# A new fixed instruction order for a fused attention and MLP-mixer kernel, made with another accounting of DMA transposes

## The chip, the core and the metric

The kernel runs on one core of a Trainium2 chip. The core has five engines that work side by side, each with an instruction queue of its own that it follows strictly in order: TensorE (PE, matrix products and transposes by the identity), VectorE (DVE), ScalarE (ACT), GpSimd (POOL) and SyncE (SP, here only for issuing transfers). Engines wait for each other by semaphores. 16 DMA engines move the data; transfers are issued by SP (queue q1 in the profile) and by POOL (queue q0). The metric is the device time of one launch in microseconds (us). Before the change the median of three runs is 201.78 us (201.45 to 202.1).

## The reference

One sequence of 2048 rows with 448 columns (bf16) goes through two blocks. LN is a layer norm without weights, over the columns of a row.

```python
# block A: 16 heads of 28 columns; each row attends to itself and to 7 earlier rows, 2 apart
off = jnp.arange(8) * 2
idx = pos[:, None] - off[None, :]                  # masked where negative
q, k, v = split(LN(x) @ wqkv)                      # 448 -> 3 x 448
logits = einsum("bhsd,bhswd->bhsw", q, k[idx]) * 28 ** -0.5
h = x + einsum("bhsw,bhswd->bhsd", softmax(logits), v[idx]) @ wo
# block B, on y = LN(h)
g = gelu(LN(y) @ w1)                               # four column quarters, shifted by +1, -1, +2, -2 rows
x1 = y + concat(shifted quarters of g) @ w2
out = h + x1 + gelu(LN(x1) @ w3) @ w4              # 448 -> 1792 -> 448
```

## The kernel before

The 2048 rows are 16 tiles of 128 rows, and these are four groups t = 0 to 3 of four tiles. Everything lives on the chip between the loads of x and the stores of the result. The phases of one group, as the code names them:

- N1 t: statistics and normalization of four tiles of x, into a buffer `lntm` (rows on the partitions; the last 64 columns are copied once more, "doubled", so that the columns fill 512).
- A1 t: `transposed` turns the buffer so that the columns lie on the partitions (`actT`), then products with wqkv give q and k. V t: products for v, evicted to `vt`; POOL then issues the copies vwp, vwa, vwb and vwc, which rearrange `vt` into the windows `vw`.
- A2 t: DVE multiplies q by shifted k (`qk_r`), PE sums over each head with a 0/1 matrix (`zc`). S t: softmax on DVE and ACT (`mx`, `ls`, `zs`, result `pb`), then PE transposes `pb`.
- A3 t: DVE builds band matrices `bd_r` from the attention weights, PE multiplies them by the `vw` windows. O t: products with wo and the residual x, written over `xin`.
- B1 t: normalization of the normalized row (two layer norms in one step), a turn, and as M t the products with w1 with gelu.
- B2 u, T u, W3 u, B3 u: products with w2, residual and layer norm; the turn; products with w3 with gelu (`h3T`); products with w4 and the store. These go by five units u of 3, 4, 4, 4 and 1 tiles.

A turn is done in one of two ways. The strings in `TURN` say which, one letter per group or unit:

- `t` (`transposed_pe`): 16 PE transposes of 128x128 by the identity, in two lots of eight, and two ACT copies of 128x1024 out of the accumulators.
- `d` (`dma_turn`): one DMA transpose, issued on SP's queue, from `lntm` to `actT`. The profile calls it `actT<-lntm`, DMA_TRANSPOSE. Before the change there are nine.

The weights w3 (1344 KB and two of 224 KB) and w4 (1568 KB) are loaded by POOL. `LOADS = '01'` puts the issue of w3 behind the last copy of V 0 and that of w4 behind the last copy of V 1, in POOL's queue only; they wait for nothing else.

The order of the work is written out. The list `ORDER` holds the number of each operation (1084 before). `_Sched.schedule` goes once through it, models a start and an end for each operation and appends it to its engine's queue. The modelled times decide only which buffer a tile gets and where filler products go on PE; what stays of the list on the chip is each engine's own order and the semaphore waits for data and buffers. Two operations on different engines keep no order of the list between them, unless one waits for the other. An edge in `op.odeps` (`behind=`) means "later in the list" and makes no wait where the engines differ or no data pass. In the model a turn is a transfer without bytes on SP, while loads and copies hold `dma_free`, the time at which modelled transfers have moved. The model also knows that certain DVE instructions and POOL's additions (`block`) delay one another.

In the profile every instruction of the program has the line 1050, where `emit_engine` calls the method of the engine (1054 in the changed kernel), so that rows are told apart by the names of their tiles: `actT<-lntm` is a turn, `arena<-in_B_w_dram` a load of a weight of block B, `vw<-vt` a copy for V, `arena<-arena,xin` on POOL the addition of the two residuals, `lntm<-xin,nm,rs_y` on DVE a normalization of bf16 rows, `ps<-ident` on PE a filler product.

Of the kernel before, what the change touches and what calls it, by code (L numbers as in the profile page):

```python
# [6 lines left out]
ALU = mybir.AluOpType  # L7
# [6 lines left out]
TURN = {'A1': 'ttdd', 'B1': 'dddd', 'B2': 'tdddt'}  # L14
NORM = {'N0': 'vavv', 'N1': 'avvv', 'B1': 'avva', 'B2': 'vaavv'}
# [6 lines left out]
    0, 9, 8, 6, 10, 1, 2, 3, 11, 4, 35, 22, 36, 5, 37, 12, 23, 38, 13, 24, 14, 25, 39, 15, 26, 46, 16, 40, 27, 52, 17, 28, 41, 53, 47, 18, 29, 55,  # L22
    48, 66, 19, 30, 42, 56, 54, 49, 20, 31, 67, 60, 57, 68, 43, 21, 32, 58, 33, 50, 61, 34, 44, 69, 51, 62, 59, 70, 63, 104, 45, 105, 64, 106, 72,
    108, 65, 73, 7, 112, 107, 111, 109, 74, 110, 75, 113, 71, 144, 142, 145, 114, 115, 124, 116, 76, 122, 117, 77, 78, 118, 120, 119, 121, 123, 148,
    143, 146, 79, 80, 81, 82, 83, 149, 147, 125, 84, 150, 126, 85, 151, 154, 155, 86, 152, 153, 87, 88, 89, 90, 91, 92, 127, 129, 133, 135, 131, 93,
    94, 130, 156, 95, 96, 140, 138, 173, 128, 161, 157, 204, 132, 205, 137, 189, 190, 248, 191, 194, 196, 250, 192, 206, 162, 163, 134, 280, 281,
    207, 282, 139, 136, 159, 158, 164, 287, 160, 195, 174, 285, 172, 209, 165, 193, 249, 166, 211, 169, 167, 170, 288, 286, 283, 175, 251, 168, 208,
    210, 171, 197, 284, 347, 252, 176, 212, 255, 97, 98, 99, 100, 101, 102, 103, 289, 199, 200, 201, 290, 254, 256, 177, 221, 219, 198, 253, 217,
    178, 257, 258, 226, 215, 260, 259, 218, 222, 141, 213, 216, 261, 179, 220, 262, 180, 263, 351, 350, 348, 349, 264, 214, 352, 181, 356, 227, 361,
    357, 359, 182, 183, 440, 369, 184, 354, 353, 225, 368, 355, 265, 185, 187, 358, 186, 188, 370, 362, 360, 372, 373, 375, 363, 224, 376, 228, 266,  # L30
    374, 231, 229, 234, 444, 232, 237, 230, 240, 267, 365, 223, 371, 233, 235, 242, 241, 236, 238, 243, 244, 294, 202, 377, 292, 203, 239, 364, 296,
    246, 268, 245, 291, 379, 247, 298, 300, 295, 299, 301, 297, 442, 269, 443, 441, 270, 303, 309, 304, 302, 381, 305, 307, 366, 445, 312, 306, 313,
    308, 271, 446, 382, 452, 454, 450, 314, 272, 315, 447, 451, 310, 560, 559, 316, 273, 317, 383, 453, 448, 367, 449, 274, 275, 561, 564, 384, 276,
    278, 457, 455, 566, 277, 279, 456, 563, 385, 319, 458, 567, 318, 327, 320, 330, 386, 321, 328, 387, 325, 388, 322, 323, 326, 333, 331, 324, 389,
    397, 336, 398, 378, 293, 380, 401, 329, 390, 334, 399, 391, 339, 335, 332, 392, 337, 393, 395, 400, 402, 394, 341, 343, 403, 396, 420, 342, 338,
    406, 404, 405, 345, 423, 421, 426, 424, 422, 407, 461, 408, 432, 425, 344, 565, 340, 410, 411, 409, 346, 427, 434, 412, 429, 428, 418, 416, 419,
    459, 460, 463, 436, 417, 430, 465, 488, 433, 489, 466, 464, 462, 467, 543, 562, 437, 431, 490, 491, 492, 497, 499, 470, 435, 471, 468, 469, 473,
    474, 494, 475, 476, 501, 438, 477, 544, 478, 498, 495, 503, 504, 505, 493, 496, 500, 502, 506, 439, 507, 518, 545, 522, 510, 509, 519, 546, 516,
    514, 512, 508, 520, 745, 515, 746, 479, 547, 480, 513, 481, 511, 521, 548, 523, 483, 517, 482, 486, 487, 549, 761, 747, 570, 311, 524, 568, 484,
    529, 531, 569, 415, 414, 572, 485, 550, 530, 748, 551, 576, 573, 528, 574, 413, 532, 577, 472, 533, 578, 575, 525, 749, 750, 751, 579, 580, 552,  # L40
    571, 526, 581, 584, 553, 762, 752, 753, 754, 755, 756, 757, 758, 763, 764, 765, 766, 767, 768, 554, 583, 582, 555, 557, 585, 556, 586, 535, 534,
    769, 536, 770, 777, 778, 779, 780, 771, 558, 590, 594, 661, 538, 587, 541, 772, 781, 664, 667, 542, 588, 539, 540, 589, 782, 773, 783, 774, 537,
    632, 668, 633, 784, 593, 592, 591, 670, 638, 636, 669, 595, 599, 662, 637, 600, 663, 634, 639, 677, 635, 665, 785, 640, 644, 666, 786, 673, 678,
    671, 759, 674, 675, 601, 676, 642, 672, 643, 641, 787, 602, 712, 775, 603, 645, 714, 604, 646, 605, 606, 610, 612, 608, 679, 614, 680, 613, 611,
    607, 615, 718, 716, 713, 715, 616, 719, 717, 720, 721, 617, 722, 623, 625, 620, 609, 649, 621, 618, 624, 650, 788, 789, 627, 619, 622, 726, 628,
    876, 908, 909, 860, 910, 630, 892, 861, 862, 893, 877, 911, 878, 912, 894, 913, 879, 863, 790, 880, 914, 864, 733, 725, 626, 724, 731, 723, 647,
    732, 651, 895, 896, 915, 916, 881, 730, 631, 653, 629, 648, 654, 734, 897, 898, 899, 735, 652, 655, 917, 865, 866, 867, 882, 900, 901, 868, 883,
    884, 885, 918, 869, 870, 871, 919, 886, 887, 888, 889, 902, 903, 904, 905, 737, 598, 597, 596, 791, 736, 776, 660, 792, 738, 727, 890, 920, 921,
    741, 891, 657, 728, 743, 872, 740, 873, 744, 739, 742, 681, 874, 682, 683, 684, 690, 922, 875, 760, 686, 685, 687, 797, 799, 795, 692, 688, 691,
    689, 906, 798, 796, 793, 800, 694, 794, 695, 801, 696, 697, 802, 803, 703, 701, 804, 699, 693, 704, 705, 849, 805, 707, 708, 698, 706, 702, 956,  # L50
    940, 806, 807, 924, 850, 810, 811, 809, 972, 973, 974, 941, 957, 925, 975, 958, 959, 960, 942, 943, 961, 962, 944, 926, 927, 945, 976, 977, 928,
    946, 710, 700, 851, 808, 812, 729, 816, 852, 815, 813, 658, 709, 711, 817, 907, 923, 527, 656, 659, 963, 929, 947, 978, 948, 979, 930, 931, 964,
    932, 933, 980, 981, 982, 983, 984, 934, 935, 985, 965, 936, 818, 937, 938, 986, 853, 854, 855, 987, 939, 949, 950, 819, 820, 966, 821, 967, 829,
    825, 827, 951, 952, 830, 822, 826, 828, 823, 824, 831, 832, 968, 833, 834, 838, 839, 840, 837, 841, 842, 953, 969, 844, 954, 970, 845, 836, 846,
    843, 835, 1020, 1068, 1021, 988, 1052, 1022, 989, 1023, 1024, 1004, 1005, 990, 1053, 1036, 1006, 991, 1007, 1069, 1037, 1038, 1008, 1054, 1055,
    1009, 992, 1056, 1057, 1010, 1039, 993, 1058, 1040, 1041, 1011, 1012, 1059, 1013, 1060, 1042, 1025, 1026, 1027, 994, 995, 1014, 1015, 847, 848,
    1028, 996, 1029, 1030, 1016, 857, 814, 1017, 1070, 1018, 971, 1019, 955, 1031, 997, 998, 1032, 1033, 999, 1034, 1000, 1061, 1001, 1071, 1072,
    1062, 1063, 1064, 1043, 1044, 1035, 1045, 1002, 1046, 1065, 1066, 1047, 1048, 1049, 1050, 1067, 1073, 1003, 1074, 1075, 1076, 1077, 1078, 1079,
    1080, 1081, 856, 1082, 1051, 1083, 858, 859]
# [125 lines left out]
class _Sched:  # L185
# [67 lines left out]
    def schedule(self, dma_bw=240.0, dma_fixed=2000.0, table_load=1300.0):  # L253
# [11 lines left out]
        free = {e: 0.0 for e in engs}  # L265
# [4 lines left out]
        dma_free = dma_land = 0.0  # L270
# [3 lines left out]
        for idx in ORDER:  # L274
            op = self.ops[idx]
# [10 lines left out]
            st = max(need, free[op.eng])  # L286
            op.t0 = st
            if op.is_dma:
# [3 lines left out]
                if op.nbytes:  # L292
                    dma_free = max(st + op.dur, dma_free) + op.nbytes / dma_bw
                    op.t1 = dma_free + dma_fixed + op.lag
                    if op.eng == "sp":
                        dma_land = max(dma_land, op.t1)
                else:
                    op.t1 = st + op.dur + op.lag + (self.SHARED if dma_free > st else 0.0)
# [14 lines left out]
            else:  # L313
# [3 lines left out]
                if op.eng == "pool":  # L317
                    waiting = op if blocked > st else None
                    st = entry = max(st, blocked)
# [81 lines left out]
def bass_sequential_preLN__sliding_local_dilated__mixer_s_mlp__prompt_kernel(  # L401
# [33 lines left out]
    with ExitStack() as es:  # L435
# [75 lines left out]
        def dve(meth, n, mode=1.0, ns=None, block=False, **kw):  # L511
            op = S.add("dve", meth, ns or (90 + n / mode) / 0.96, 205.0, **kw)
            op.block = block
            return op
# [121 lines left out]
        def normalize(kind, i, out_ap, in_ap, summed=False, norm="v"):  # L636
# [6 lines left out]
            if summed:  # L643
                return dve("tensor_scalar", D, ns=421.0 if kind == 2 else 307.0, out=out_ap, in0=in_ap, scalar1=nm[:, kind, i:i + 1],
                           scalar2=rs, op0=ALU.add, op1=ALU.mult)
            return dve("tensor_scalar", D, ns=421.0 if kind == 2 else 307.0, out=out_ap, in0=in_ap, scalar1=mv[:, kind, i, 0:1],
                       scalar2=rs, op0=ALU.subtract, op1=ALU.mult)
# [166 lines left out]
        def phase_V(t):  # L814
# [10 lines left out]
            if t > 0:  # L825
                dma("vwp%d" % sl, vw[0:PADK, sl, 0, :], vt[112:128, 1 - sl, 3, :], PADK * 1024, 600.0, "pool")
# [265 lines left out]
```

## Time and profile before

| | us |
|---|---|
| median of three runs | 201.78 (201.45 to 202.1) |
| the profiled execution, whole | 199.47 |
| its span, first to last instruction | 197.7 |
| PE busy | 185.4 |
| ACT busy | 139.8 |
| DVE busy | 123.2 |
| POOL busy | 47.5 |
| mean granted TensorE clock | 1.000 |

The profiled execution is one of its own: it is 2.31 us below the median, and 1.77 us of it lie outside the span. Busy times are sums over an engine's instructions; engines overlap. PE's idle time, 12.3 us, is the span less its busy time. Times on a timeline count from the start of the span.

The nine turns, from issue to landing (us): 23.69 to 28.64 (A1 2), 31.28 to 42.69 (A1 3), 56.54 to 61.02 (B1 0), 85.06 to 89.34, 100.27 to 104.55, 113.62 to 118.02, 135.38 to 139.64, 138.48 to 142.76, 163.28 to 167.55.

### The profile page before, as it was taken

How to read it: one execution, taken by the hardware profiler on the slowest of the kernel's cores; microseconds unless marked ns; L12 is line 12 of the kernel's file. 1: busy time of each engine (PE TensorE's matmuls, PEld its weight loads, DVE VectorE, ACT ScalarE, POOL GpSimd, SP SyncE). 2: the span in 40 equal slices, each digit the busy share in tenths (PEclk: the TensorE clock that was granted, in tenths of full speed). 3: DMA queues.
4: the chain of work that ended last, by engine and by line, in shares of the span. 5: the costliest groups of instructions: out<-in, count | busy, mean ns of one | idle time of the engine just before them, and what ended most of it. 6: DMA issues, size and time to landing. Idle time of an engine off the chain costs nothing.

```text
span 197.7 us, 3964 instructions
## 1 busy us (share of the span) xinstructions
PE 185.4 (94%) x1594; PEld 89.0 (45%) x1594; DVE 123.2 (62%) x222; ACT 139.8 (71%) x315; POOL 47.5 (24%) x96
## 2 busy tenths in 40 slices
PE   6899999949988998999979999999999999999995
PEld 2554333424333445554534554445544445444553
DVE  5989889996999989967995684400335050302024
ACT  4749997977799979999639979699144993067011
POOL 6594080044100000400930010430400009520000
PEclk9999999999999999999999999999999999999999
DMA  5976099973882000250350060004910006100013
GB/s 163 325 221 200 5 203 308 146 169 85 232 227 48 3 0 3 69 109 0 60 109 7 0 111 0 3 0 78 203 46 3 0 2 153 46 3 23 0 35 104
DMA packets 26546, 17.32 MB, mean 88 GB/s; under 512 B 19904, under 2 KB 24960, under 8 KB 26528
## 3 DMA queue, kind: packets, MB, share of 16 engines
q1 hardware_dynamic: 24448, 9.77, 22.3%
q0 software_dynamic: 2080, 7.31, 13.7%
q8 instruction: 12, 0.20, 0.4%
q14 instruction: 6, 0.05, 0.1%
HBM read 7.91 MB, written 1.84 MB: 49 GB/s over the span
## 4 chain that ended last, share of the span: by engine, by line
PE 76%; DMA 9%; DVE 8%; ACT 4%; issue 1%; SPq 0%; ACTq 0%
PE ps L1050 76%; DMA actT<-lntm 8%; DVE lntm L1050 3%; ACT lntm L1050 2%; DMA xin<-in_A_x_dram 1%; ACT arena L1050 1%; DVE arena L1050 1%; DVE mx L1050 1%; ACT actT L1050 1%; DVE ls L1050 1%; DVE zs L1050 1%; DVE st L1050 1%; SPq L1050 0%; DVE pb L1050 0%; ACT ls L1050 0%
## 5 line engine op out<-in xcount | busy, mean ns | idle before, releaser
L1050 PE MATMUL ps<-actT,arena 128*128 128x512 bf16 (+4 forms) x348 | 68.9, 364 | 2.8 <-DMA actT<-lntm 2.6
L1050 PE MATMUL ps<-arena,h3T 128*128 128x448 bf16 (+1 forms) x238 | 46.7, 342 | 0.0
L1050 PEld LDWEIGHTS ps<-actT,arena 128*128 128x128 bf16 (+1 forms) x348 | 27.8, 97 | 38.9 <-issue 6.5
L1050 ACT ACTIVATE h3T<-ps 128x512 bf16<-128x512 f32 (+1 forms) x56 | 28.2, 576 | 23.4 <-PE ps L1050 23.4
L1050 ACT ACTIVATE arena<-ps 128x512 bf16<-128x512 f32 (+5 forms) x64 | 31.5, 520 | 11.6 <-PE ps L1050 11.0
L1050 DVE TENSOR_TENSOR qk_r<-arena 128x4096 bf16<-128x4096 bf16 (+1 forms) x16 | 32.0, 2016 | 1.2 <-PE ps L1050 1.2
L1050 PEld LDWEIGHTS ps<-arena,h3T 128*128 128x128 bf16 x238 | 22.7, 98 | 20.6 <-issue 1.9
L1050 DVE SCALAR_TENSOR_TENSOR ost<-ps,mrs,arena 128x448 bf16<-128x448 f32 (+1 forms) x17 | 10.8, 653 | 30.9 <-PE ps L1050 28.8
L1050 POOL TENSOR_TENSOR arena<-arena,xin 128x448 f32<-128x448 f32 x16 | 16.4, 1048 | 41.5 <-DVE lntm L1050 23.0
L1050 POOL DMA_DIRECT2D vw<-vt x15 | 9.0, 603 | 55.2 <-ACT vt L1050 39.2
L1050 ACT ACTIVATE actT<-ps 128x512 bf16<-128x512 f32 (+2 forms) x25 | 15.7, 654 | 7.8 <-PE ps L1050 7.7
L1050 DVE TENSOR_TENSOR bd_r<-arena,bmask 80x2048 bf16<-80x2048 bf16 x16 | 18.7, 1215 | 3.1 <-ACT arena L1050 3.1
L1050 DVE BATCH_NORM_STATS2 st<-xin 128x6 f32<-128x448 bf16 x24 | 14.3, 615 | 2.9 <-ACT xin L1050 1.8
L1050 DVE SCALAR_TENSOR_TENSOR arena<-xin,rs_y,ps 128x448 f32<-128x448 bf16 x16 | 10.5, 677 | 8.7 <-PE ps L1050 8.7
L1050 PE MATMUL ps<-wo_s,actT 128*128 128x448 bf16 x64 | 14.8, 354 | 0.8 <-ACT actT L1050 0.8
L1050 PE MATMUL ps<-actT,w_s 128*112 128x512 bf16 (+1 forms) x64 | 14.5, 386 | 1.0 <-DMA actT<-lntm 1.0
L1050 ACT ACTIVATE lntm<-arena,nm 128x448 bf16<-128x448 f32 x16 | 10.5, 660 | 5.3 <-DVE nm L1050 5.3
L1050 PE MATMUL ps<-w_s,arena 112*128 112x448 bf16 x64 | 13.8, 353 | 0.3 <-ACT arena L1050 0.3
L1050 PE MATMUL ps<-arena,actT 128*128 128x448 bf16 (+1 forms) x64 | 12.4, 354 | 0.5 <-ACT arena L1050 0.5
L1050 POOL TENSOR_TENSOR rs_y<-rs_x,mhalf 128x4 f32<-128x4 f32 (+1 forms) x5 | 4.7, 937 | 25.7 <-DVE rs_x L1050 25.6
L1050 DVE COPY lntm<-lntm 128x256 bf16<-128x256 bf16 (+2 forms) x16 | 3.3, 207 | 12.0 <-ACT lntm L1050 11.6
L1050 PEld LDWEIGHTS ps<-actT,w_s 128*112 128x112 bf16 (+1 forms) x64 | 6.6, 128 | 6.8 <-DMA actT<-lntm 1.4
(73 smaller groups left out, 193.9 us busy)
## 6 DMA issues: line engine op xcount, KB each, us to landing
out_dram<-ost SPq DMA_DIRECT2D x15, 112.0 KB, 1.8
arena<-in_B_w_dram POOLq DMA_DIRECT2D x1, 1568.0 KB, 10.1
arena<-in_B_w_dram POOLq DMA_DIRECT2D x1, 1344.0 KB, 9.7
vw<-vt POOLq DMA_DIRECT2D x4, 320.0 KB, 3.8
vw<-vt POOLq DMA_DIRECT2D x4, 256.0 KB, 7.3
xin<-in_A_x_dram SPq DMA_DIRECT2D x2, 448.0 KB, 5.6
xin<-in_A_x_dram SPq DMA_DIRECT2D x3, 224.0 KB, 4.8
arena<-in_A_wqkv_dram SPq DMA_DIRECT2D x1, 672.0 KB, 4.6
```

What stands on the lines that cost most here:

```text
L1050: inst = getattr(eng, meth)(**kw)
```

## The change

The constants that steer the search, the model in `schedule`, and the order found with it are changed.

```diff
-TURN = {'A1': 'ttdd', 'B1': 'dddd', 'B2': 'tdddt'}
-NORM = {'N0': 'vavv', 'N1': 'avvv', 'B1': 'avva', 'B2': 'vaavv'}
+TURN = {'A1': 'ttdd', 'B1': 'tddd', 'B2': 'tdddt'}
+NORM = {'N0': 'vavv', 'N1': 'vvvv', 'B1': 'avva', 'B2': 'vaavv'}
...
 ORDER = [
-    0, 9, 8, 6, 10, 1, 2, 3, 11, 4, 35, 22, 36, 5, ...
+    0, 9, 8, 6, 7, 10, 1, 2, 3, 11, 4, 35, 22, 36, ...
...
                 else:
-                    op.t1 = st + op.dur + op.lag + (self.SHARED if dma_free > st else 0.0)
+                    free["sp"] = max(st + op.dur, dma_free + self.SHARED) + self.SHARED if dma_free > st else st + op.dur
+                    op.t1 = free["sp"] + op.lag
...
             if summed:
-                return dve("tensor_scalar", D, ns=421.0 if kind == 2 else 307.0, out=out_ap, ...
...
+            op.block = kind != 2
+            return op
...
             if t > 0:
-                dma("vwp%d" % sl, vw[0:PADK, sl, 0, :], vt[112:128, 1 - sl, 3, :], PADK * 1024, 600.0, "pool")
+                dma("vwp%d" % sl, vw[0:PADK, sl, 0, :], vt[112:128, 1 - sl, 3, :], PADK * 1024, 600.0, "pool", behind=rest)
```

- The model's turn: where other transfers are still moving at its start, SP counts as busy until they have moved, and somewhat longer, and the turn ends accordingly. `free["sp"]` and `op.t1` are numbers of the model; no wait is emitted for them.
- `op.block = kind != 2`: DVE normalizations of bf16 rows (block A and B1) and POOL's additions exclude each other in the model.
- `behind=rest` on vwp: this copy stands in the list behind POOL's set-up work and first loads.
- `TURN['B1']`: the turn of B1 0 goes from a DMA to PE, with 16 transposes and two ACT copies. Eight DMA turns are left, and 1087 operations in all. The edited letter of `NORM['N1']` is not read, since group 0 goes by `N0`.
- `ORDER` is another list throughout, so every engine's queue is in another order. Four places that the prediction names: POOL now issues vwa0, vwc0, 224 KB of w3, vwa1, 224 KB of w3, vwb0, vwp1, vwb1, vwc1, the main part of w3, w4 and then vwp2, where before w4 came behind vwa2 of group 2, which waits for PE. In DVE's queue the last copy of N1 3, which the A1 3 turn waits for, stands behind half of the first `qk_r` of A2 1 and two steps of S 0. Two tiles' statistics stand ahead of the first normalization. POOL's additions of B2 0, three in a row before, stand apart from one another, between the powers. Two filler products are added on PE ahead of the last four transposes (T 4).

## The prediction

> **What bounds the kernel now.** I read the page's busy times and its chain first, then the chain in order of time, then the timelines of TensorE (PE), GpSimd (POOL) and VectorE (DVE) around every idle stretch of PE, and last the DMA queues. The page:
>
> ```profile
> span 197.7 us, 3964 instructions
> PE 185.4 (94%) x1594; PEld 89.0 (45%) x1594; DVE 123.2 (62%) x222; ACT 139.8 (71%) x315; POOL 47.5 (24%) x96
> ...
> PE 76%; DMA 9%; DVE 8%; ACT 4%; issue 1%; SPq 0%; ACTq 0%
> ```
>
> PE is busy 185.4 of 197.7 us, so only its idle 12.3 us can be won, while nothing caps a loss. The chain in order of time and PE's timeline (start, duration, what; idle before and its releaser in brackets) show where PE stands still:
>
> ```profile
> 31.28 11.40 DMA actT<-lntm
> 42.69 0.14 issue
> 42.82 7.61 PE ps L1050 x137
> ...
> 56.54 4.48 DMA actT<-lntm
> 61.02 0.04 issue
> 61.07 4.75 PE ps L1050 x64
> ```
>
> ```profile
> 1.59 4.32 PE L1050 MATMUL ps<-ident 128*128 128x512 bf16 x13 [1.59 <-POOL epsilon L1050]
> ...
> 39.83 0.43 PE L1050 MATMUL ps<-bd_r,vw 80*32 80x64 bf16 x32
> 42.82 0.81 PE L1050 MATMUL ps<-actT,arena 128*128 128x512 bf16 x3 [2.56 <-DMA actT<-lntm]
> ...
> 104.28 0.64 PE L1050 MATMUL ps<-ident,pb 128*80 128x128 bf16 x8 [1.86 <-DVE pb L1050]
> ```
>
> The three large gaps after the start are 2.56 us (turn of A1 3), 0.97 us at 61.07 (turn of B1 0; its chain step is shown above) and 1.86 us (pb of S 3). Five smaller ones between 52 and 76 us make 1.89 us (0.25, 0.51, 0.34, 0.18, 0.61). From 104.28 to 195.0 PE has no gap.
>
> Why the A1 3 turn took 11.4 us, where the quickest takes 4.3, is in GpSimd's queue and the DMA packets of 31.6 to 35.9 us:
>
> ```profile
> 24.60 1.77 POOL L1050 DMA_DIRECT2D vw<-vt  x3 [7.73 <-ACT vt L1050]
> 26.36 0.77 POOL L1050 DMA_DIRECT2D arena<-in_B_w_dram  x1
> 27.12 1.28 POOL L1050 DMA_DIRECT2D vw<-vt  x2
> 28.40 0.55 POOL L1050 DMA_DIRECT2D arena<-in_B_w_dram  x1
> ...
> 48.39 1.11 POOL L1050 DMA_DIRECT2D arena<-in_B_w_dram  x1
> ```
>
> ```profile
> q0 software_dynamic: 240, 1.12, 101.8%
> ...
> actT<-lntm SPq DMA_TRANSPOSE x1, 11.4
> ```
>
> The turn was issued at 31.28, yet until 35.9 only packets of q0 (POOL's queue) move; its own packets (q1) come when q0 has run dry. The transfers issued before it (w3's main part, 1344 KB, at 26.36; vw copies; 224 KB of w3) landed until 39.54, and the turn 3.15 us later. The other way round, a 16 KB vw copy issued at 24.60, just behind the turn of 23.69, landed only at 28.34. So transfers are served in the order of their issue, across queues. w4 (1568 KB) was issued at 48.39 and landed at 58.47; the B1 0 turn (issued 56.54) landed 2.38 us after the last POOL transfer (58.64).
>
> Last, S 3:
>
> ```profile
> 94.83 3.23 DVE L1050 TENSOR_SCALAR lntm<-xin,nm,rs_y 128x448 bf16<-128x448 bf16 x2
> ```
>
> ```profile
> 95.82 3.12 POOL L1050 TENSOR_TENSOR arena<-arena,xin 128x448 f32<-128x448 f32 x3
> ```
>
> Two normalizations took 1.05 and 2.25 us beside POOL's additions; undisturbed they take 0.39. They stand in DVE's queue ahead of S 3's ls, whose pb releases PE at 104.28.
>
> **The change, part by part.** The edits of the planner (the turn's end, `op.block`, `behind=rest`) emit no instruction; they act through ORDER alone, which fixes each engine's own queue. In the list the A1 3 turn stands before w3's main part and w4, but on POOL nothing makes these two wait.
>
> *POOL's queue.* It becomes vwa0, vwc0, 224 KB of w3 (behind ACT's last eviction of V 0, about 23.8), vwa1 (behind an eviction of V 1, about 25.1), 224 KB of w3, vwb0, vwp1, vwb1, vwc1, w3 main, w4; only then comes a wait on PE. At the rows' 0.53 to 1.1 us per issue the last goes out near 31. w4 thus moves from 48.39 to about 30, ahead of the A1 3 turn.
>
> *Turn A1 2.* It goes out near 24.6 (before 23.69) with vwa0 and vwc0, 304 KB, ahead. 2448 KB landed between 28.34 and 39.54, 219 KB/us; so 1.4 us more, and it lands near 30.3, where PE wants it at 29.4. PE waits 0 to 1.5 us, I take 1.0; it is inside the next term.
>
> *Turn A1 3.* Its last DVE copy now stands behind half of qk_r (2.28), zs (0.68) and the reciprocal (0.55): issue near 34.8 instead of 31.28. Queued between the two turns are 224+256+224+320+16+320+48+1344+1568 = 4320 KB, or 4.42 MB. They begin landing where the vwp copy landed before (28.34), 0.9+1.4 us later: 30.6. The packets of 31.6 to 35.9 ran at 260 GB/s: 17.0 us, so 47.6; the turn lands 2.38 to 3.15 us later, 50.4. Bounds: the best stretch, 283 GB/s (28.0 to 31.2), gives 48.6; 219 KB/us with 3.15 gives 53.5. I take 260, a window with nothing but such packets. PE's queue is in order, so all behind that product waits too. PE goes on near 50.6 instead of 42.82: **+7.8** (5.9 to 10.8).
>
> *PE's clock after the stop.* The stop is some 9.5 us, and no gap in this trace is longer than 2.56. After 2.56 PE ran at once at its usual pace. After the idle start it didn't: the first seven of the 13 products of 128x512 start 0.427 us apart, the later ones 0.213, though the granted clock reads 1.00. That is 7 x 0.214 = 1.5 us lost. Bounds 0 and 1.5; the stop is several times the harmless gap, so I take **+1.5**. [...]
>
> *What catches up.* While PE stands, DVE and ACT finish what they can (the next qk_r and bd products). The five small gaps behind it, 1.89 us, are waits on them: between 0 and -1.9, I take **-0.9**.
>
> *Turn B1 0 on PE.* The 0.97 us goes; 16 transposes of 128x128 come (4 take 0.23 us start to start, 8 take 0.71: 0.9 to 1.4 us), and two ACT copies (about 1.05 each) ahead of M 0. ACT has time after the stop: **0** (-0.1 to +0.5, and to +2.5 if PE must wait for both copies).
>
> *S 3.* POOL's additions no longer stand together: one comes early, the others between powers. The two normalizations fall back to 0.39, saving 2.5 us of DVE against a gap of 1.86. **-1.5** (-1.86 to 0, as one other normalization may meet an addition).
>
> *The rest.* Start: two more stats ahead of the first normalization, +0.2 (-0.1 to +0.5), hidden in the wait for the A1 3 turn. The two filler products before T 4 (0.43 us) fit before its transposes, whose inputs come from DVE; without that cover +0.4. After 104 us PE has the same work, while the turns of B1 2 and T 1 came only 0.14 to 0.2 us early: 0, and up to +3 if one is late.
>
> Sum: 7.8 + 1.5 - 0.9 + 0 - 1.5 = +6.9. The profiled execution took 199.47 (span 197.7 and 1.77 around it); the median of the runs is 201.78, 2.31 above. So 206.4 in the profile and **208.7** as a median.
>
> **The rivals.**
> *The turn doesn't wait for what is queued* (faster). If the DMA engines alternate between q1 and q0, the turn of 34.8 needs its 4.3 us and its 2.6 us of packets a second time: 41.7. PE goes on at 41.9 instead of 42.82, -0.9; with S 3 (-1.5) and the small gaps (-0.2) that is -2.6: 196.9 in the profile, 199.2. It decides if the turn lands before about 44. Against it: no q1 packet in 4.6 us after issue. After w3's packets (7168 bytes) q0 went on with vw's (4096 bytes), so even the change of transfer didn't let the turn in. [...] Chance 0.14.
> *w4 isn't really queued ahead*: POOL's issue blocks, or the DMA engines take in only part of q0 ahead of a turn. 22 packets of 4480 bytes per engine behind 12 of 7168 are more than the trace has held at once. Then 2752 KB (2.82 MB) lie ahead: 30.6 + 10.8 + 2.8 = 44.2, PE +1.5; minus 1.5 (S 3) and 0.5 (gaps): 201.3, within 200 to 203. Chance 0.13 (0.07 faster, 0.02 same).
> *The stop and a second loss*: a later turn of B1 or T late, or PE waiting for B1 0's copies, +3: 211.7. The slack of 0.14 us speaks for it, ACT's head start against. Chance 0.11.
> That the change doesn't do what its words say (turns behind other transfers by the list, transfers ahead of turns on the chip) is my forecast itself: chance 0.62, its own range 206 to 211.
>
> **How the numbers follow.** About 0.3% (0.6 us) can be told from no change. Faster: 0.14 + 0.07 = 0.21. Same: 0.02, and 0.01 from the edge of my own case. Slower: 0.62 + 0.04 + 0.11 - 0.01 = 0.76. The range leaves out the first rival and the top of the third: 200.5 to 212.
>
> **What would show it.** In the profile after: w4 issued by GpSimd near 30; the A1 3 turn issued near 35 and landing near 50; PE idle some 9.5 us there and slow for some 2.7 us after it; no normalization of 2.25 us near 95; a gap before S 3's pb under 0.5. The forecast is wrong if w4 goes out late or the turn lands before 44. It is too high if POOL's transfers run faster than 283 GB/s.

## The result

The changed kernel takes 211.47 us (median of six runs, 210.54 to 212.99), the kernel before 201.49 in runs beside it: ratio 1.051, 95% interval 1.046 to 1.057, or 9.2 to 11.5 us slower. The forecast was 208.7, slower. The direction and the kind of loss were right. The turn that paid was not the one that I named, nor by the rule that I gave. Of thirteen executions of the kernel before that were taken beside the first experiments, three with a mean granted clock of 1.00 took 199.65 to 200.45 us, seven with 0.991 took 201.57 to 202.39, and three with 0.983 took 204.06 to 205.58; its profile is of the first kind.

The page of the changed kernel (the clock row has 40 slices of 5.3 us, 9 is 90% or more of full speed), and its chain:

```profile
span 211.3 us, 4006 instructions
PE 190.3 (90%) x1612; PEld 90.9 (43%) x1612; DVE 121.1 (57%) x222; ACT 141.4 (67%) x317; POOL 46.1 (22%) x96
PEclk9999997559999999999999999999999999999999
```

```profile
25.02 17.90 DMA actT<-lntm
42.92 0.05 issue
42.97 6.28 PE ps L1054 x19
```

PE's timeline and POOL's around it (start, duration, what; idle before and its releaser in brackets):

```profile
28.80 1.05 PE L1054 MATMUL ps<-qk_r,zc 128*32 128x512 bf16 x16
42.97 8.31 PE L1054 MATMUL ps<-actT,arena 128*128 128x512 bf16 x28 [13.12 <-DMA actT<-lntm]
```

```profile
24.01 1.19 POOL L1054 DMA_DIRECT2D vw<-vt  x2 [6.83 <-ACT vt L1054]
25.19 0.55 POOL L1054 DMA_DIRECT2D arena<-in_B_w_dram  x1
25.73 0.64 POOL L1054 DMA_DIRECT2D vw<-vt  x1
26.36 0.56 POOL L1054 DMA_DIRECT2D arena<-in_B_w_dram  x1
26.91 2.37 POOL L1054 DMA_DIRECT2D vw<-vt  x4
29.27 1.88 POOL L1054 DMA_DIRECT2D arena<-in_B_w_dram  x2
```

w3's main part and w4 go out at 29.27 to 31.15, as forecast. But the turn of the chain, 17.90 us from issue to landing, is that of A1 2, not of A1 3: issued at 25.02, 1.0 us behind the first copy. PE stands 13.12 us for it; the granted clock falls to half at 34.5, 4.65 us after PE's last product. The A1 3 turn takes longer still (35.65 to 54.43), yet costs nothing, because PE, late by then, comes to it only at 56.52.

The window from 43.0 to 48.2 us shows the second loss; the columns are the stretch, its length, PE's busy time and products, the granted clock (1.00 is full speed), the DMA engines' busy share and GB/s:

```profile
43.00:48.20 5.20, 5.20 (x12) 0.50 1.00 335
```

Twelve products of 128x512 start 0.427 us apart instead of 0.213: 2.6 us.

The sum for the profiled execution (212.99 us, span 13.6 above that of before): stop 13.1, half clock 2.6, B1 0's transposes 0.9, the end 1.3, the smaller gaps 0.6, the start 0.4; less the gaps that are gone, 2.56 (A1 3), 0.97 (B1 0) and 1.86 (S 3). That makes 13.5 of 13.6. At the end it is 4.0 us from the last product with w4 to the end of the span instead of 2.7: DVE stands 1.36 for a store ahead of T 4's last copy. Seven smaller gaps make 2.94 us, where six made 2.35. At the start the 13 filler products take 5.73 us instead of 4.32, and the last products ahead of the stop begin at 28.80; in the kernel before they begin at 28.43, behind the same work.

S 3's part came as forecast. The group of those normalizations (min/median/max in ns), where 2250 stood before:

```profile
L1054 DVE TENSOR_SCALAR lntm<-xin,nm,rs_y x8: 383/391/745, 28.7 to 111.7; 128x448 bf16<-128x448 bf16 x8
```

### The profile page after: what moved, and what is told of

It reads as the page before. It is cut to its first block, busy times and chain, and to the rows that moved or that the text cites. A ratio compares the mean times of both kernels' runs of the same rounds, so it can differ in the third digit from the quotient of the medians.

```text
span 211.3 us, 4006 instructions
## 1 busy us (share of the span) xinstructions
PE 190.3 (90%) x1612; PEld 90.9 (43%) x1612; DVE 121.1 (57%) x222; ACT 141.4 (67%) x317; POOL 46.1 (22%) x96
## 4 chain that ended last, share of the span: by engine, by line
PE 57%; ACT 16%; DVE 15%; DMA 10%; issue 1%; POOL 0%; DVEq 0%; POOLq 0%; ACTq 0%
PE ps L1054 57%; DMA actT<-lntm 8%; ACT arena L1054 6%; DVE bd_r L1054 5%; DVE qk_r L1054 4%; ACT vt L1054 3%; ACT lntm L1054 2%; DVE st L1054 2%; ACT actT L1054 2%; DMA out_dram<-ost 2%; DVE lntm L1054 1%; DVE arena L1054 1%; DVE ost L1054 1%; ACT L1049 1%; ACT L1054 1%
## 5 line engine op out<-in xcount | busy, mean ns | idle before, releaser
L1054 PE MATMUL ps<-actT,arena 128*128 128x512 bf16 (+4 forms) x348 | 71.1, 373 | 13.1 <-DMA actT<-lntm 13.1
L1054 PEld LDWEIGHTS ps<-actT,arena 128*128 128x128 bf16 (+1 forms) x348 | 28.3, 98 | 51.2 <-DMA actT<-lntm 13.6
L1054 PE MATMUL ps<-arena,h3T 128*128 128x448 bf16 (+1 forms) x238 | 47.2, 342 | 0.0
L1054 DVE TENSOR_TENSOR bd_r<-arena,bmask 80x2048 bf16<-80x2048 bf16 x16 | 19.5, 1266 | 18.4 <-ACT arena L1054 18.4
L1054 ACT ACTIVATE actT<-ps 128x512 bf16<-128x512 f32 (+2 forms) x27 | 17.4, 674 | 16.9 <-PE ps L1054 16.7
L1054 DVE BATCH_NORM_STATS2 st<-xin 128x6 f32<-128x448 bf16 x24 | 13.7, 610 | 0.6 <-DMA xin<-in_A_x_dram 0.6
L1054 PE MATMUL ps<-ident 128*128 128x512 bf16 x21 | 7.9, 536 | 1.6 <-POOL epsilon L1054 1.6
```

Source lines behind the costliest of these rows:

```text
L1054: inst = getattr(eng, meth)(**kw)
```

## The experiments

All changes of order below touch POOL's queue alone, and the other engines' queues stay as they are, unless it is said otherwise. `_behind(op, ...)` moves operations in ORDER to right behind `op`. A line with `deps.add` adds a real wait. The numbers: 198, 200, 199 are vwa0, vwc0, vwb0; 289 is vwp1; 290, 291, 292 are vwa1, vwb1, vwc1; 203 and 202 the 64-row loads of w3, 201 its main part, 293 is w4; 350 and 443 are the turns of A1 2 and A1 3. Theory Q is the rule of my prediction, that what was issued earlier moves first. Theory S is that a turn shares the DMA engines with what is in hand beside it.

### Are w3 and w4 the cause?

```diff
+_behind(380, 201, 293)          # 380: vwp2, which waits for PE
```

> The changed kernel, with the main part of w3 and w4 (2912 KB) moved in POOL's queue behind vwp2, which waits for PE; nothing else differs. Theory Q (queue: what is handed in early delays a turn until it has moved, and w3 and w4 are the cause): the A1 2 turn, which took from 25.02 to 42.92 us in the changed kernel, lands by 32, PE stands under 2.5 us for it, and the time falls by about 13 to near 198. Theory S (sharing: a turn whose packets meet POOL's vw copies and the 64-row parts of w3 crawls along with them, whatever stands behind these in POOL's queue): the A1 2 turn still lands at 41 to 43, PE still stands 11 to 13 us, the A1 3 turn lands some 6 us earlier than its 54.43 but PE isn't there yet, and the time stays within 2 us of the changed kernel, 209.5 to 212.

213.02 us, ratio 1.059 (1.049 to 1.068): no better than the changed kernel. With 2912 KB out of the way until 60 us, the A1 2 turn is no earlier: it landed at 47.01, and PE stood 17.31 us, in a trace of the slowest of the four executions (215.75; the others took 212.28 to 213.67). So S's figures were missed too (41 to 43, 209.5 to 212). The chain of this kernel, and a window inside the turn:

```profile
24.91 22.10 DMA actT<-lntm
47.01 0.05 issue
```

```profile
28.50:40.00 11.50, 1.24 (x18) 0.73 1.16 66
```

The DMA engines' busy share was 1.16, but all that was in hand moved only 66 GB/s. The copy vwa1, 256 KB, issued at 25.62, landed at 40.30. Q has fallen for this turn: its wait isn't the bytes of the weights. What is in hand beside it are the vw copies and the 64-row loads.

### Both turns kept clear

```diff
+_behind(103, 198, 200, 199)     # 103: POOL's last load of the start
+_behind(443, 290, 289, 291, 292, 203, 202, 201, 293)
...
+        S.ops[198].deps.add(S.ops[350])
+        S.ops[290].deps.add(S.ops[443])
```

> The changed kernel, with both early turns kept clear of POOL's transfers: vwa0, vwc0 and vwb0 wait for the landing of the A1 2 turn, and the copies for group 1, all of w3, and w4 wait for the landing of the A1 3 turn. Both theories: both turns take 4.3 to 4.9 us; the one of A1 2 lands near 29.4 and PE stands under 0.5 us for it; that of A1 3 lands near 39.5 and PE doesn't wait; no half clock; the three gains forecast for the change (A1 3's 2.56, B1 0's 0.97 and S 3's 1.86 us less 1.2 us of added transposes and filler) show: 195 to 199, faster than the kernel before by 1 to 3 per cent. If instead it is no faster than the kernel before, the new order has another loss that the stop at A1 2 had covered.

202.60 us, ratio 1.005 (1.001 to 1.010): 9 us regained, but not faster than before. The turns took 4.36 and 5.27 us, as expected. PE still stood 5.03 us ahead of A1 3's first product, though the turn had landed at 40.91: an eviction of V 2 came at 46.05.

```profile
46.10 1.46 PE L1066 MATMUL ps<-actT,arena 128*128 128x512 bf16 x3 [5.03 <-ACT vt L1066]
```

It overwrites the buffer that vwp1 reads, and I had held vwp1 back with the rest. This loss is of my own making, not of the new order. So vwp1 goes forward:

```diff
+_behind(103, 198, 200, 199, 289)
+_behind(443, 290, 291, 292, 203, 202, 201, 293)
```

> As the kernel that keeps both turns clear, where PE then stood 5.03 us, not for the turn (landed 40.91) but for an eviction of V 2 that had to wait until the copy vwp1 (16 KB), held back with the others, had read the buffer. Here vwp1 goes with the first group, behind the A1 2 turn's landing. Theory S: both turns take 4.3 to 5.3 us, that stop and the half clock behind it (1.5 to 2.6 us) are gone: 194 to 197, 2 to 4 per cent faster than the kernel before. Rival: with the stop gone DVE or ACT is what PE waits for, and less than half of the 7 us come out: 198.5 to 201.

**197.54 us, ratio 0.987 (0.983 to 0.992): some 6 per cent below the changed kernel and 0.8 to 1.7 per cent below the kernel before.** That is less than was expected (194 to 197, 2 to 4 per cent): by the two ratios 3.6 us came out of the 7 that the stop and the half clock seemed to cost, near the rival's bound of half. Turns, clock and span:

```profile
L1066 SPq DMA_TRANSPOSE actT<-lntm x8: 1742/1902/2767, 24.6 to 161.8; - x8
...
DMA to landing us min/median/max: 4.3/4.3/4.8
```

```profile
core 0: 196.1 us, clock 1.000
```

The same eleven transfers, handed in 4 to 5 us later (three copies and vwp1) and 13 to 17 us later (the rest), are worth 13 to 14 us.

### What the loads do, and what the lead does

```diff
+_behind(103, 198, 200, 199, 201, 293)
+_behind(443, 290, 289, 291, 292, 203, 202)
...
+        S.ops[198].deps.add(S.ops[350])
+        S.ops[290].deps.add(S.ops[443])
```

> As the kernel that keeps both turns clear, but the main part of w3 and w4 (2912 KB) are issued right behind vwb0, so that they are in flight when the A1 3 turn is issued near 35, and no vw copy and no 64-row part of w3 is. Theory Q: the turn waits until they have moved: from about 33, 2.98 MB at 260 GB/s is 11.5 us, and 2.4 to 3.2 us more: it lands near 47, PE stands some 6.5 us, the time is 203 to 206. Theory S (weight loads and a turn take turns packet by packet on the DMA engines, and only the copies make it crawl): it lands at 39.5 to 42, PE stands under 2 us, the time is within 2 us of the kernel that keeps both turns clear.

208.46 us, ratio 1.037 (1.030 to 1.044). The turn landed at 46.14, where Q said 47 and S 39.5 to 42. So S was too kind to the loads: the turn landed 4.1 us past the latest it allowed. (PE stood until 51.27 instead, again for V 2's eviction behind vwp1, so that the time by itself says nothing here.) Of the changed kernel, the window from 44 to 51 us, in which the A1 3 turn ran beside w3's main part and w4, shows how the two moved; the queues' packets, MB and share:

```profile
DMA packets 961, 2.59 MB, mean 370 GB/s; under 512 B 495, under 2 KB 496, under 8 KB 961
...
q0 software_dynamic: 482, 2.47, 93.4%
q1 hardware_dynamic: 479, 0.12, 8.0%
```

The 479 packets of q1 are the turn's (256 bytes each), and 465 of the 482 of q0 are the loads' (4480 or 7168): nearly one for one, at 370 GB/s. The turn has 2048 packets, so that in these 7 us it got on by less than a quarter. That is not so in every window: in this experiment's own trace, from 39.2 to 44.6 us, 1028 packets of q1 moved beside 296 of q0.

```diff
+        S.ops[198].deps.add(S.ops[254])     # 254: ACT, ended at 26.2 us
```

> The changed kernel with one wait added: the first of POOL's copies, vwa0, also waits for the second ACTIVATE of N1 3's sums (near 26.2 us), so that POOL's chain begins about 1.2 us behind the A1 2 turn (25.02) instead of 1.0 ahead of it; its order is untouched. Theory S: what counts is whether the copies are on the DMA engines when the turn comes: the A1 2 turn lands within 5.5 us (by 30.5), PE waits under 1.5 us there; the A1 3 turn of 35.3 then meets w3's main part and w4 and lands at 45 to 48 as beside these loads alone, PE stands 4 to 7 us: 202 to 205. Rival: the copies slow the turn although they come later, the landing is past 35, and the time within 3 us of the changed kernel.

206.74 us, ratio 1.034 (1.030 to 1.038). POOL's chain, its order untouched, began at 26.26, 1.7 us behind the turn's issue at 24.57, and the A1 2 turn took 4.40 us. In the changed kernel it began 1.0 us ahead, and the turn took 17.90. The price passed to the next turn, as expected in kind but dearer (48.69 instead of 45 to 48, and a time of 202 to 205 had been expected):

```profile
35.09 13.60 DMA actT<-lntm
48.69 0.05 issue
48.74 6.97 PE ps L1055 x103
```

PE stood 8.22 us, and the clock was halved again (a mean of 0.975 over the span). This is the stop that I had forecast (9.5 us at A1 3): it is there as soon as the A1 2 turn is spared.

The kernel before, with vwc1 and w4 handed in early:

```diff
+_behind(202, 292, 293)
```

> The kernel before, with vwc1 and w4 (1568 KB) moved in POOL's queue to right behind the 224 KB of w3 that is issued at 28.40 us: w4 goes out near 29.5 instead of 48.39 and is in flight when the A1 3 turn is issued at 31.28. Theory Q: w4's 6.6 us are added to that turn's landing: 49.3 instead of 42.69, PE stands 9 us instead of 2.56, and half clock costs 1.5 to 2.6 more: slower by 3 to 4 per cent, 208 to 210. Theory S: in POOL's queue w4 stands behind the copies that slow this turn, so that it meets only the turn's tail: the turn lands at 42.5 to 45, the time is 0 to 2.5 us above the kernel before.

216.46 us, ratio 1.075 (1.066 to 1.084): dearer than either theory said.

```profile
31.64 26.12 DMA actT<-lntm
57.76 0.14 issue
```

Until 44 the turn's packets and those of POOL's transfers moved nearly one for one (314 of q1, 342 of q0 from 37.2 to 44.0); w4 landed at 47.74. But PE had not stopped before 40.6, and its last product released POOL's next three transfers at 40.94: vwp2, 64 rows of w3, and vwb1. These met the turn's remainder; the last of them landed at 57.58, the turn at 57.76. Neither theory had reckoned with transfers that come behind a turn while it is still held up. Here a delayed turn collected three more transfers.

### Copies or half-filled loads?

The best version, with only one kind handed in around the A1 3 turn; 182 is a DVE step that ends 0.7 us before the turn, and the wait of vwa0 for the A1 2 turn stays. In both traces the first transfer went out 0.40 us ahead of the turn, the others 0.2 to 0.9 us behind it.

```diff
+_behind(103, 198, 200, 199, 289, 290, 291, 292)
+_behind(443, 203, 202, 201, 293)
...
+        S.ops[290].deps.add(S.ops[182])
+        S.ops[203].deps.add(S.ops[443])
```

> What makes a turn crawl? The best version so far (both turns clear, 197.5 us), with only the three copies of group 1 (vwa1, vwb1, vwc1: 624 KB from chip memory to chip memory) handed in about 1 us ahead of the A1 3 turn (near 35.1) instead of behind its landing. Theory S1 (a turn crawls beside copies from chip memory): it takes over 9 us and lands past 44, PE stands over 3 us, the time rises by 3 or more. Theory S2 (bytes: the turn takes its share beside them): 624 KB are 2.4 us at 260 GB/s; it lands by 40 to 42.5, PE stands under 2 us, the time rises by 0 to 2.

202.42 us, ratio 1.005 (1.001 to 1.009). The turn took 9.89 us and landed at 45.01, and PE stood 4.50. 624 KB would be 2.4 us at 260 GB/s; they cost the turn 5.1 beyond the best version's 4.80. S1's figures came. But 260 GB/s was the pace of a window in which more than half of the bytes were w3's. By themselves the copies were slower: in the best version the four of the first group, 640 KB, went out from 29.32 on with no turn beside them, and the last (issued at 31.15) landed at 35.08:

```profile
29.32 2.35 POOL L1066 DMA_DIRECT2D vw<-vt  x4 [12.09 <-DMA actT<-lntm]
```

```profile
vw<-vt POOLq DMA_DIRECT2D x1, 16.0 KB, 3.9
```

That is 5.8 us in all, some 114 GB/s. So the turn paid no more than the copies take by themselves, and a slowing beyond that the run doesn't show.

```diff
+_behind(103, 198, 200, 199, 289, 203, 202)
+_behind(443, 290, 291, 292, 201, 293)
...
+        S.ops[203].deps.add(S.ops[182])
+        S.ops[290].deps.add(S.ops[443])
```

> The same, with the two 64-row loads of w3 (448 KB, from the chip's main memory) in place of the copies: handed in about 1 us ahead of the A1 3 turn, everything else for group 1, and w3's main part and w4, behind its landing. S1: no crawl, the turn lands by 40 to 42 and the time stays within 2 us of 197.5. S2: 1.7 us at most are added, 40 to 42 as well. Rival S3 (what crawls beside a turn are transfers that fill only half the partitions, copies and loads alike): the turn takes over 8 us and lands past 43.

197.35 us, ratio 0.978 (0.971 to 0.985), not told apart from the best version. The turn took 7.06 us (landed 42.28, by its edge outside S1's and S2's 42), and PE stood 1.68. 448 KB cost 2.3 us, near their bytes (1.8). S3's figures (over 8, past 43) didn't come: the copies from chip memory to chip memory were the dearer company here (5.1 us for 624 KB). They differ from the loads also in packet size (4096 against 7168 bytes) and number, which no run separates.

Neither run is the crawl of the changed kernel, where both kinds and a turn were in hand together: its nine transfers took 21.3 us, from 24.01 to the last landing at 45.32. The same nine took 12.2 in the run with the copies later (26.26 to 38.46), mostly without a turn. With 4.4 us for the turn that would be 16.6, so by this estimate some 4.7 us were lost by being in hand together. Why, no run shows.

### The other steps of the sum

PE kept busy in the stop (54 identity products ahead of the waiting one, operation 351; the only change in PE's queue):

```diff
+        hot = S.ops[351]
+        bank = [t.slot for t in hot.tiles if t.pool.name == "bank"][0]
+        warm_ = _Op(len(S.ops), hot.prio, "pe", filler(bank, 54), 0.0, 0.0)
+        warm_.deps = {d for d in hot.deps if not d.is_dma}
...
+        order["pe"].insert(order["pe"].index(hot), warm_)
```

> The changed kernel with 54 products of the identity (128x512, 0.216 us each, 11.6 us) put on PE ahead of the product that waits 13.12 us for the A1 2 turn; nothing else differs, the turn lands as late. If the 12 products that start 0.427 us apart behind the stop are slow because PE stood still (the granted clock reads 0.50 there), they now start 0.213 apart, the granted clock stays near 1.00 and the time falls by 2.0 to 2.6 us, 1.0 to 1.2 per cent below the changed kernel, 209 against 211.5. If they are slow for another reason, such as the transfers still running, the time stays within 0.5 us of the changed kernel.

209.06 us, ratio 1.045 (1.040 to 1.049), against 1.051. Between medians that is 2.4 us, by the two ratios 1.3; the intervals overlap. The trace settles it. The same window as above, with nearly as many bytes moving:

```profile
43.00:48.20 5.20, 4.80 (x25) 1.00 1.06 320
```

From A1 2's first product to the one behind S 0's transposes it is 7.86 us, against 10.40 in the changed kernel. The turn is as late as there (18.24 us), so the half clock is the stop's doing, and it cost 2.5 us.

S 3 alone, on the kernel before:

```diff
+_behind(526, 415, 414, 413)     # three additions, behind a power
```

> The kernel before, with only the three POOL additions that ran from 95.82 to 98.94 us moved behind the power that ended at 102.66. My prediction's step: the two normalizations of 1.05 and 2.25 us fall to 0.39 each, pb comes 2.5 us earlier, PE's gap of 1.86 us before it goes to under 0.4, and the time falls by 1.5 (0.7 per cent; 0 to 1.9). Rival: something else is as late as pb (the turn of B1 2, 0.2 us later, or the additions now beside DVE's reciprocal and pb), and under 0.5 us comes out.

199.32 us, ratio 0.992 (0.987 to 0.996): 1.7 us, between 0.8 and 2.6. PE's gap ahead of pb is gone, and the longest of the normalizations takes 557 ns instead of 2250.

The turn of B1 0 as a DMA again, in the best version (this shifts the numbers by three; PE and ACT lose the transposes and copies):

```diff
+ORDER[:] = [n if n <= 317 else n - 3 for n in ORDER if n not in (318, 319, 320)]
+TURN['B1'] = 'dddd'
```

> The best version so far, with the turn of B1 0 as a DMA again (no 16 transposes and two ACT copies, nothing else moved). My prediction's step: both ways cost the same within 0.5 us. Theory S: near 56 us, when this turn is issued, w4 is still moving (landed 59.97 in the best version) with copies behind it that land until 61.59, so the DMA turn lands at 62 or later instead of 60.3, and M 0, wanted near 60, waits: 1.5 to 4 us slower than the best version. If it is as fast, the change of TURN did nothing for the time.

202.37 us, ratio 1.004 (1.000 to 1.008), by the ratios 3.4 us above the best version:

```profile
55.64 7.40 DMA actT<-lntm
63.04 0.04 issue
```

PE stood 5.02 us for it. Beside w4 and the copies behind it the DMA turn was dear here, and the one on PE, with 0.9 us of transposes in the changed kernel, wasn't.

The cure without the new order:

```diff
+_behind(289, 199, 200, 198)
+_behind(440, 290, 201, 202)     # 440: the A1 3 turn of the kernel before
...
+        S.ops[290].deps.add(S.ops[440])
```

> The kernel before, old order and all, with the same cure: in POOL's queue only the copies for group 0 and vwp1 stay ahead of the A1 3 turn; vwa1, w3's main part and 224 KB of w3 wait for its landing. Theory S: that turn takes 4.3 to 5.5 us instead of 11.4, lands by 37, PE's gap of 2.56 us goes, and the time falls by 2.0 to 2.6 us (ratio 0.987 to 0.990): as much as the new order with both turns clear (0.987), so that the new order by itself is worth no more than the difference. Rival: the old order has a wait right behind that gap, and under 1 us comes out.

198.82 us, ratio 0.987 (0.981 to 0.992), the same as the best version of the new order. The turn took 4.28 us and the gap of 2.56 is gone. Between the two traces, both with a mean clock of 1.00, that is 1.6 us of span (196.1 instead of 197.7); the ratio is some 2.7 us. The rest fits the clock: ten of the eleven runs of the kernel before beside this one read 0.99, and four of this one's six read 1.00. No trace shows in which stretch those runs had the half clock. S 3's gap is still there (1.85), so its gain could perhaps be added.

## Why the prediction was right, and where it was wrong

- **The number**: 211.47 lies in the range of 200.5 to 212, but above the 206 to 211 of my own case, and it is near 208.7 partly by luck. From profile to profile I forecast +6.9 (206.4) and 212.99 was measured, +13.5. I had added 2.31 us to come from the profile of before to its median. Some 1.8 of it goes with the clock: the profile read 1.00, and the executions with 0.991 took that much longer. The changed kernel reads 0.967 to 0.968 in all six runs, and its profile lies 1.5 above its median, not 2.31 below.
- **POOL's queue** (w4 at about 30): right. The early hand-in of the chain as a whole is the loss. But "w4 ahead of the A1 3 turn" was not the part that hurt first, since the run without the early w3 and w4 was as slow.
- **Served in the order of their issue**: this rule failed, and with it the split between the turns. I had it from two rows of before, and one of them spoke against it: the 16 KB copy issued behind the A1 2 turn landed at 28.34, ahead of the turn (28.64). What the traces of four kernels give in its place: from the issue of the A1 3 turn to its first packet, 226 packets of POOL's queue moved in the kernel before, 240 in the one with the loads beside, 238 in the one with the copies later, 253 in the one with the early w4; that is 14 to 16 for each of 16 DMA engines. So behind transfers that had been coming for 4 us or more, some fifteen packets per engine, as a mean, went ahead of the turn in these four traces, and what stood further back shared with it. That lead was 3.9 to 5.5 us; with nothing ahead, in the best version, the first packet came after 1.2 to 1.3. Where the first transfer was only 0.40 us old, 64 packets of copies or 47 of loads went ahead. In the kernel before only 65 packets stood further back, which looked like strict order.
- **Turn A1 2, 0 to 1.5 us, I take 1.0**: wrong by 12. I priced the 304 KB ahead of it by their bytes and let what came behind it cost nothing. It met 1264 KB of copies and 448 KB of loads and landed in the midst of them.
- **Turn A1 3, +7.8**: in the changed kernel nothing, because PE came later than it. Such a stop did come in the run with the later copies (8.22 us). That the two wrong terms, +13.1 in one place and 0 in the other, leave a time near the forecast is luck.
- **PE's clock, +1.5**: right in kind, too small, 2.5 to 2.6. I capped it by the start of the trace. In the changed kernel the granted clock read 0.50 from 34.5 on, 4.65 us into the stop, and came back at 48.2, 5.2 us after PE went on. In five other traces with a stop of 4.50 us or more (loads beside, copies later, early w4, copies beside, B1 0 by DMA) the granted clock fell to half 1.8 to 5.0 us into the stop, the earliest beside the copies and the latest with the early w4, and came back 2.8 to 5.0 us after PE went on. After the 2.93 us ahead of A1 3 in the S 3 run and the 2.56 of before the traces show no half clock. So neither of the two lengths is a fixed one here, and that a gap of 2.56 is harmless is read from one execution only.
- **What catches up, -0.9**: wrong, the smaller gaps were 0.6 us larger in sum. DVE and ACT ran dry too: DVE stood 16.1 us, since its next step needed products from behind the stop.
- **Turn B1 0, 0**: right, 0.9 us of transposes for a gap of 0.97. That it would have cost 5 us as a DMA in the cleared order I did not see.
- **S 3, -1.5**: right, 1.7 (0.8 to 2.6) by itself.
- **The rest, 0**: 1.7 us too low, 1.3 at the end and 0.4 at the start.
- **The rival of alternating queues** (0.14): its rule came nearer than mine, its time did not. The 482 and 479 packets of the changed kernel agree with it, the 296 and 1028 of the run with the loads beside do so less. What the rival's 41.7 left out are the packets that go ahead and the copies' slower pace.

## What to carry to other kernels

Look for what is in hand on the DMA engines when a transfer on the critical path goes out, not only for what was issued on its queue. Here two waits that hold POOL's transfers back until a DMA transpose has landed were worth 13 us. With the same cure the old order came to the same ratio as the new one (0.987 both), so the search for a new order brought nothing that can be told beyond it. The planner's list by itself held nothing back on the chip: w3's main part and w4 went out at 29.27 to 31.15, ahead of the A1 3 turn of 35.65, which the list puts before them. So ask of each such order whether an engine really waits for it. When transfers are held back, ask which buffers they read, since one 16 KB copy held back too long stopped PE for 5 us. And look at the granted clock of every run before a profile is set against a median.

## What the runs showed of the hardware

- A DMA transpose of 4.3 us by itself took 9.9 us beside 624 KB of copies from chip memory to chip memory, and 17.9 and 22.1 beside the longer chains of copies and half-filled loads (in one window inside the latter, all that was in hand moved 66 GB/s at a DMA busy share of 1.16). In one window with main-memory loads 479 of the transpose's packets moved beside 482 of theirs, at 370 GB/s, in another 1028 beside 296. Copies by themselves took 5.8 us for 640 KB.
- 2.7 us made the difference: with copies begun 1.0 us ahead of it the transpose took 17.9 us, with copies begun 1.7 us behind it 4.4.
- PE at half clock for 5.2 us after a stop of 13 us, and at full clock where it was kept busy with idle products. In six traces the granted clock fell 1.8 to 5.0 us into a stop.
